# Feed-forward layer behind attention: low parts on VectorE, x split in chunk pairs, high parts first

## Chip, cores and metric

One core of one Trainium2 chip. The metric is the device time of one execution in microseconds (us); 1079.61 us is the median of three runs of the kernel before (1079.18 to 1080.98). Its engines: TensorE (PE, matmuls), VectorE (DVE), ScalarE (ACT), GpSimd (POOL), and SyncE (SP), which issues DMAs.

## The reference

Windowed attention with a few global tokens, then two feed-forward layers over the same 2176 tokens of width 512:

```python
x = attention(q_l, k_l, v_l, q_g, k_g, v_g)      # 4 batches x (32 global + 512 local) tokens, 8 heads x 64
# layer 1 (1536 wide)
xn = x / sqrt(mean(x * x, -1) + 1e-6) * rms_g
g, val = xn @ w_gate, xn @ w_val
x = (g / (1 + exp(-g)) * val) @ w_out
# layer 2 (2048 wide)
h = x @ w_in
P = a[0] + a[1]*h + a[2]*h**2 + a[3]*h**3
Q = 1 + abs(b[0])*abs(h) + abs(b[1])*h**2
out = (P / (Q + 1e-6)) @ w_out2
```

The weights come as 64-bit floats, the rest as 32-bit.

## The kernel before

**Precision.** Each matmul of the two layers is done in a reduced 32-bit format (F32R), three times: high part of the weight by high part of x, low by high, high by low. A high part is a rounding copy on ScalarE, a low part a subtraction (value less high part) on VectorE or GpSimd. TensorE so has three matmuls for each product, lines 618 to 620 for the way up and 645 to 647 for the way down.

**Weights.** `Weights.stages` (line 73) turns a 128x512 tile of 64-bit words into a high and a low part in four stages: ScalarE L83 and L85, VectorE L91, L92 and L95, GpSimd L99 (an add of two 32-bit tiles), then ScalarE L104 and a low part L105 on the engine `lo_eng` that the caller of `step` passes: GpSimd in attention and in layer 2, VectorE between them. A tile is fetched by SyncE one conversion ahead. Twelve tiles of layer 2 are converted in layer 1 and stored to a scratch in DRAM; GpSimd's queue loads them back (L70) when layer 1 is over.

**Layer 1** (`FFN1`) runs as 24 tasks: three groups of 512 of the 1536 middle features, and in each the eight blocks of 288 or 256 tokens (half a batch). A task splits x of its block into four chunk tiles `xt0` to `xt3` of one buffer each, high (L607, ScalarE) and low (L608), then goes through four slices k of 128 features. For each it has `up` of chunks 0 and 1, `up` of chunks 2 and 3 (12 matmuls each, with a `yield` behind: a unit), and `act`: silu or tanh on ScalarE, the product with the value half on VectorE (L633), its high part `ah` (L634, ScalarE) and low part `al` (L636). The way down of the block before (`down`, 12 matmuls for each of four output slices m) stands behind slices 0 and 1; its result goes to `y`, by ScalarE (L651) in group 0, by an addition on VectorE (L653) later. The split for the next task is asked for behind the last `up` of the last slice. Low parts of x are on GpSimd in group 0 and on VectorE in groups 1 and 2; `al` is on GpSimd while the gate is computed with tanh, and on VectorE once silu's table is in use (unit 96 on).

`norm_stages` scales x of a block beforehand; its three adds (L578, L580, L582) are GpSimd's. The eight norms are appended in the attention loop at the ends of steps 4, 8, 14, 18, 22, 26, 30 and 34, and each step takes three stages of them, which is one whole norm.

**Order.** The attention loop (line 854) interleaves the first 60 units with its steps t = 0 to 35: `target` says how many should be done, 7 at the end of step 8, 60 at the end. `between` and the loop behind a step run units up to that. Then the rest of layer 1 runs unit by unit, from unit 72 on with a conversion step behind each. Layer 2 (`ffn2`) follows, with VectorE, ScalarE and GpSimd (L130, L741) in its middle.

The emitted instructions are put in order by a planner that simulates the engines: among the instructions that are ready it takes the one emitted first, and `high_priority(offset=n)` counts an instruction as emitted n places sooner. Each engine runs its instructions in the order so found. PSUM has five banks for `psg` and `psv` behind attention and three for `psA` and the norms.

Of the kernel before, what the change touches and what calls it, by code (L numbers as in the profile page):

```python
# [10 lines left out]
F32 = mybir.dt.float32  # L11
F32R = mybir.dt.float32r
I32 = mybir.dt.int32
U32 = mybir.dt.uint32
AF = mybir.ActivationFunctionType
# [14 lines left out]
NB1 = SG + SL // 2  # L30
# [11 lines left out]
class Weights:  # L42
# [30 lines left out]
    def stages(self, job, lo_eng, r8_act):  # L73
        nc = self.nc
        self.fetch(job)
        key, raw, alloc, _, scratch = job
        v = self.pool.tile([128, 512], I32, tag="cv", name=f"cv{self.n}", bufs=2)
        self.n += 1
        vf = v.bitcast(F32)
        if self.wide:  # L80
            words = raw.rearrange("p a f -> p (a f)").rearrange("p (f w) -> p f w", w=2)
            hi, lo = words[:, :, 1], words[:, :, 0]
            nc.scalar.activation(out=vf, in_=hi.bitcast(F32), func=AF.Abs)  # L83
            if r8_act:
                nc.scalar.activation(out=lo, in_=lo.bitcast(U32), func=AF.Copy, scale=2.0**-29)  # L85
            else:
                nc.gpsimd.tensor_scalar(
                    out=lo, in0=lo.bitcast(U32), scalar1=2.0**-29, scalar2=1.0, op0=ALU.mult, op1=ALU.mult
                )
            yield  # L90
            nc.vector.tensor_scalar(out=vf, in0=vf, scalar1=TINY, scalar2=None, op0=ALU.max)  # L91
            nc.vector.tensor_scalar(  # L92
                out=v, in0=v, scalar1=3, scalar2=0x3FFFFFFF, op0=ALU.logical_shift_left, op1=ALU.bitwise_and
            )
            nc.vector.scalar_tensor_tensor(  # L95
                out=v, in0=hi, scalar=-0x40000000, in1=v, op0=ALU.bitwise_and, op1=ALU.bitwise_or
            )
            yield
            nc.gpsimd.tensor_tensor(out=v, in0=v, in1=lo, op=ALU.add)  # L99
        else:  # L100
            nc.vector.tensor_copy(vf, raw[:, 1].bitcast(F32))
        yield
        out = alloc("w", F32R)
        nc.scalar.activation(out=out[:, 0], in_=vf, func=AF.Copy)  # L104
        lo_eng.tensor_tensor(out=out[:, 1], in0=vf, in1=out[:, 0].bitcast(F32), op=ALU.subtract)  # L105
        if scratch is None:
            self.ready[key] = out
        else:
            nc.sync.dma_start(out=scratch, in_=out.bitcast(I32))
# [424 lines left out]
class FFN1:  # L534
# [4 lines left out]
    LN2H = 0.34657359027997264  # L539

    def __init__(self, tc, pool, x, y, gam, wts):
        self.nc, self.pool, self.x, self.y, self.gam, self.wts = tc.nc, pool, x, y, gam, wts
        nc = self.nc
        self.ones = pool.tile([128, 128], F32, name="ones")
        nc.gpsimd.memset(self.ones, 1.0 / DM)
        self.eps = pool.tile([128, 1], F32, name="eps")
        nc.gpsimd.memset(self.eps, self.LN2H * (127 - 0.0430))
        self.norms = {}
# [21 lines left out]
    def norm_stages(self, blk):  # L570

        nc = self.nc
        nb = self.width(blk)
        t = lambda i: self.pool.tile([128, NB1], F32, tag=f"st{i}", name=f"st{i}_{blk}", bufs=1)[:, :nb]
        m, r, u = t(0), t(1), t(2)
        nc.scalar.activation(out=m, in_=self.xs(blk, 0), func=AF.Square)
        nc.scalar.activation(out=r, in_=self.xs(blk, 1), func=AF.Square)
        nc.gpsimd.tensor_tensor(out=m, in0=m, in1=r, op=ALU.add)  # L578
        nc.scalar.activation(out=u, in_=self.xs(blk, 2), func=AF.Square)
        nc.gpsimd.tensor_tensor(out=m, in0=m, in1=u, op=ALU.add)  # L580
        nc.scalar.activation(out=r, in_=self.xs(blk, 3), func=AF.Square)
        nc.gpsimd.tensor_tensor(out=m, in0=m, in1=r, op=ALU.add)  # L582
        yield
        ps = self.bank(self.acc, f"psN{blk}")
        nc.tensor.matmul(ps[:, :nb], self.ones, m, start=True, stop=True)
        nc.vector.tensor_scalar(out=m, in0=ps[:, :nb], scalar1=1e-6, scalar2=None, op0=ALU.add)
        nc.scalar.activation(out=r, in_=m.bitcast(I32), func=AF.Exp, scale=-self.LN2H / 2**23, bias=self.eps)
        yield
        for up in (1.0 + 1.65e-4, 1.0):
            nc.vector.scalar_tensor_tensor(out=u, in0=r, scalar=-0.5 * up, in1=m, op0=ALU.mult, op1=ALU.mult)  # L590
            nc.vector.tensor_tensor(out=u, in0=u, in1=r, op=ALU.mult)
            nc.vector.scalar_tensor_tensor(out=r, in0=u, scalar=1.5 * up, in1=r, op0=ALU.add, op1=ALU.mult)
        for c in range(4):
            v = self.xs(blk, c)
            nc.vector.scalar_tensor_tensor(out=v, in0=v, scalar=self.gam[:, c : c + 1], in1=r, op0=ALU.mult, op1=ALU.mult)

    def split(self, grp, blk):
        nc = self.nc
        if grp == 0:
            for _ in self.norms[blk]:  # L600
                pass
        lo = nc.gpsimd if grp == 0 else nc.vector
        nb = self.width(blk)
        xt = [self.pool.tile([128, 2, NB1], F32R, tag=f"xt{c}", name=f"xt{grp}_{blk}_{c}", bufs=1)[:, :, :nb] for c in range(4)]
        for c in range(4):
            v = self.xs(blk, c)
            nc.scalar.activation(out=xt[c][:, 0], in_=v, func=AF.Copy)  # L607
            lo.tensor_tensor(out=xt[c][:, 1], in0=v, in1=xt[c][:, 0].bitcast(F32), op=ALU.subtract)  # L608
        return xt

    def up(self, k, blk, xt, cs, pss):
        nc = self.nc
        for c in cs:
            for j in range(2):
                w = self.wts.get(("gv"[j], k))
                wh, wl = (w[:, i, c * 128 : c * 128 + 128] for i in range(2))
                ps = pss[j][:, : self.width(blk)]
                nc.tensor.matmul(ps, wh, xt[c][:, 0], start=(c == 0), stop=False)  # L618
                nc.tensor.matmul(ps, wl, xt[c][:, 0], start=False, stop=False)  # L619
                nc.tensor.matmul(ps, wh, xt[c][:, 1], start=False, stop=(c == 3))  # L620

    def act(self, k, blk, pss, use_silu):
        nc = self.nc
        nb = self.width(blk)
        t = lambda tag, dt, bufs: self.pool.tile([128, NB1], dt, tag=tag, name=f"{tag}{blk}_{k}", bufs=bufs)[:, :nb]
        a, ah, al = t("a", F32, 2), t("ah", F32R, 6), t("al", F32R, 5)
        g, v = pss[0][:, :nb], pss[1][:, :nb]
        if use_silu:
            self.last_silu = nc.scalar.activation(out=a, in_=g, func=AF.Silu)  # L629
        else:  # L630
            nc.scalar.activation(out=a, in_=g, func=AF.Tanh, scale=0.5)
            nc.vector.scalar_tensor_tensor(out=a, in0=a, scalar=1.0, in1=g, op0=ALU.add, op1=ALU.mult)  # L632
        nc.vector.scalar_tensor_tensor(out=a, in0=a, scalar=1.0 if use_silu else 0.5, in1=v, op0=ALU.mult, op1=ALU.mult)  # L633
        nc.scalar.activation(out=ah, in_=a, func=AF.Copy)  # L634
        lo = nc.vector if use_silu else nc.gpsimd
        lo.tensor_tensor(out=al, in0=a, in1=ah.bitcast(F32), op=ALU.subtract)  # L636
        return ah, al

    def down(self, grp, blk, acts, m):
# [15 lines left out]
    def units(self, tasks):  # L655

        prev, xt = None, None
        for i, (grp, blk, use_silu) in enumerate(tasks):
            if xt is None:
                xt = self.split(grp, blk)  # L660
            acts = []
            for kk in range(4):
                k = 4 * grp + kk
                pss = [self.bank(self.gv, f"ps{j}_{blk}_{k}") for j in "gv"]
                self.up(k, blk, xt, (0, 1), pss)
                yield
                self.up(k, blk, xt, (2, 3), pss)
                if kk == 3:
                    xt = self.split(*tasks[i + 1][:2]) if i + 1 < len(tasks) else None
                acts.append(self.act(k, blk, pss, use_silu()))  # L670
                yield
                for m in ((0,), (1, 2, 3), (), ())[kk]:
                    if prev:
                        self.down(*prev, m)
                        yield
            prev = (grp, blk, acts)
        for m in range(4):
            self.down(*prev, m)
            yield
# [89 lines left out]
def kernel(  # L769
# [83 lines left out]
    ffn.set_psum(pp, ("big", banks[0]), ("o", banks[2]))  # L853
    for t in range(LAST + 1):
        if t >= SECOND:
            target[0] = 7 + (IN_ATTN - 7) * (t + 1 - SECOND) / (LAST + 1 - SECOND)
        elif t >= START:
            target[0] = 7 * (t + 1 - START) / (SECOND - START)
        with tc.high_priority(offset=50) if t >= START else nullcontext():
            att.step(t, between)  # L860
        while done[0] < target[0] - 1:
# [25 lines left out]
    wb = left("wb")  # L887
    pp = ps_scope.enter_context(tc.tile_pool(name="ps2", bufs=1, space=PSUM))
    ffn.set_psum(pp, ("gv", 5), ("acc", 3))
    for f in group_loads(1, wb):  # L890
        f()
    norms += [ffn.norm(blk) for blk in ORD if blk not in ffn.norms]
# [80 lines left out]
```

## Time and profile before

| | us |
|---|---|
| median of 3 runs | 1079.61 |
| the profiled execution | 1080.32 |
| its span, first to last instruction | 1078.5 |
| TensorE busy | 1002.8 (93%) |
| VectorE busy | 792.1 (73%) |
| ScalarE busy | 597.6 (55%) |
| GpSimd busy | 368.0 (34%) |

The last output of attention (L413) starts at 307.6 us, the first silu (L629, group 1) at 380.5, the last at 676.7. Busy time is a union over the instructions of an engine, and a matmul counts from its start to a modelled end, so a busy TensorE is not a TensorE at its peak: the row says when it had something to do. [...] In the views of waits, "A <- B" is an idle time of A's engine that ended when B was done. A low mean clock together with a full busy share means that matmuls ran, but slowly.

### The profile page before, as it was taken

Reading aid. Unit: us, or ns where it says so; the run is one execution under the profiler, and the core shown is the slowest. Engines: PE = TensorE matmul, PEld = TensorE weight load, DVE = VectorE, ACT = ScalarE, POOL = GpSimd, SP = SyncE. Lnnn points to the kernel's source line nnn. Section 1 sums busy time; section 2 is a strip of 40 time slices with the busy share of each in tenths; the row PEclk is TensorE's granted clock in tenths of the full one; section 3 lists DMA queues with packets and bytes.
Section 4 is the critical chain, followed back from the end, with each engine's and each line's share of the span. In section 5 each row is a group of like instructions: output and inputs, shape, how many; then the busy total and the mean of one; then the engine's idle time right before and its main releaser. Section 6 shows DMA issues by size and latency. Waiting matters only on the chain.

```text
span 1078.5 us, 23732 instructions
## 1 busy us (share of the span) xinstructions
PE 1002.8 (93%) x9376; PEld 906.2 (84%) x9376; DVE 792.1 (73%) x1754; ACT 597.6 (55%) x1347; POOL 368.0 (34%) x401
## 2 busy tenths in 40 slices
PE   4588999999989989999999999999999999999997
PEld 3366777878878889899989999888989889898895
DVE  3566455565559998863896453799898998989987
ACT  2645454556557664543664242566666666666674
POOL 2445212212227533310331011454353443534443
PEclk8878999999999999999999999999999999999999
DMA  8833545454152422530431013400000000000000
GB/s 220 241 89 70 137 98 122 109 122 92 43 208 87 157 79 78 198 136 2 157 117 41 1 40 118 156 1 1 30 1 30 1 1 30 1 30 2 1 30 20
DMA packets 104047, 83.45 MB, mean 77 GB/s; under 512 B 63360, under 2 KB 91008, under 8 KB 103936
## 3 DMA queue, kind: packets, MB, share of 16 engines
q1 hardware_dynamic: 102208, 75.64, 24.2%
q0 software_dynamic: 1728, 6.29, 1.8%
q8 instruction: 74, 1.21, 0.5%
q14 instruction: 37, 0.30, 0.1%
HBM read 62.64 MB, written 10.75 MB: 68 GB/s over the span
## 4 chain that ended last, share of the span: by engine, by line
PE 38%; DVE 15%; ACT 4%; DMA 2%; issue 2%; POOL 2%; ACTq 0%; POOLq 0%; SPq 0%; DVEq 0%
PE psH L715 4%; PE psH L717 4%; PE psB L750 4%; PE psH L716 4%; PE psB L751 4%; PE psB L752 3%; DVE q L725 2%; PE psg L620 2%; DVE q L737 2%; DVE r L738 2%; PE psg L618 2%; PE psg L619 2%; PE psv L618 2%; PE psv L620 2%; PE psv L619 2%
## 5 line engine op out<-in xcount | busy, mean ns | idle before, releaser
L130 POOL TENSOR_SCALAR gh<-p 128x384 fp32r<-128x384 f32 (+1 forms) x96 | 58.0, 604 | 210.0 <-DVE p L739 179.6
L715 PE MATMUL psH<-yt,w_h 128*128 128x384 f32 (+1 forms) x384 | 126.1, 329 | 0.9 <-ACT yt L697 0.7
L716 PE MATMUL psH<-yt,w_h 128*128 128x384 f32 (+1 forms) x384 | 125.5, 328 | 0.0
L717 PE MATMUL psH<-yt,w_h 128*128 128x384 f32 (+1 forms) x384 | 123.6, 328 | 0.9 <-DVE yt L698 0.9
L645 PE MATMUL psA<-ah,w_o 128*128 128x288 f32 (+1 forms) x384 | 113.8, 298 | 9.1 <-ACT ah L634 3.1
L618 PE MATMUL psg<-xt,w_g 128*128 128x288 f32 (+1 forms) x384 | 115.7, 302 | 5.7 <-ACT xt L607 4.9
L620 PE MATMUL psg<-xt,w_g 128*128 128x288 f32 (+1 forms) x384 | 114.2, 298 | 5.3 <-DVE xt L608 4.7
L618 PE MATMUL psv<-xt,w_v 128*128 128x288 f32 (+1 forms) x384 | 113.5, 296 | 0.5 <-DVE a L632 0.4
L750 PE MATMUL psB<-w_p,gh 128*128 128x512 f32 x272 | 108.2, 398 | 5.5 <-POOL gh L130 5.4
L619 PE MATMUL psg<-xt,w_g 128*128 128x288 f32 (+1 forms) x384 | 112.7, 293 | 0.0
L647 PE MATMUL psA<-al,w_o 128*128 128x288 f32 (+1 forms) x384 | 111.7, 292 | 0.4 <-DVE al L636 0.4
L619 PE MATMUL psv<-xt,w_v 128*128 128x288 f32 (+1 forms) x384 | 112.1, 292 | 0.0
L620 PE MATMUL psv<-xt,w_v 128*128 128x288 f32 (+1 forms) x384 | 111.7, 292 | 0.0
L646 PE MATMUL psA<-ah,w_o 128*128 128x288 f32 (+1 forms) x384 | 111.2, 291 | 0.0
L741 POOL TENSOR_TENSOR gl<-p,gh 128x384 fp32r<-128x384 f32 (+1 forms) x96 | 108.3, 1128 | 8.4 <-PE psB L752 0.4
L751 PE MATMUL psB<-w_p,gh 128*128 128x512 f32 x272 | 107.3, 394 | 0.0
L735 ACT ACTIVATE r<-q,cq 128x384 f32<-128x384 f32 (+1 forms) x96 | 57.4, 598 | 63.9 <-DVE q L725 63.0
L725 DVE SCALAR_TENSOR_TENSOR q<-q,bv,t 128x384 f32<-128x384 f32 (+1 forms) x96 | 69.7, 726 | 21.1 <-ACT q L723 20.9
L645 PEld LDWEIGHTS psA<-ah,w_o 128*128 128x128 f32 x384 | 73.2, 191 | 12.5 <-ACT ah L634 3.8
L752 PE MATMUL psB<-w_p,gl 128*128 128x512 f32 x272 | 82.3, 395 | 0.0
L633 DVE SCALAR_TENSOR_TENSOR a<-a,psv 128x256 f32<-128x256 f32 (+1 forms) x96 | 41.5, 433 | 54.4 <-ACT a L629 47.8
L620 PEld LDWEIGHTS psg<-xt,w_g 128*128 128x128 f32 x384 | 73.8, 192 | 8.9 <-DVE xt L608 6.9
(173 smaller groups left out, 2808.1 us busy)
## 6 DMA issues: line engine op xcount, KB each, us to landing
vw<-vw SPq DMA_DIRECT2D x64, 130.0 KB, 2.5
raw_h<-in_moe_w_in_dram SPq DMA_DIRECT2D x16, 512.0 KB, 3.9
raw_p<-in_moe_w_out_dram SPq DMA_DIRECT2D x16, 512.0 KB, 4.7
raw_g<-in_moe_w_gate_dram SPq DMA_DIRECT2D x12, 512.0 KB, 5.8
raw_v<-in_moe_w_val_dram SPq DMA_DIRECT2D x12, 512.0 KB, 5.6
raw_o<-in_moe_w_out_dram SPq DMA_DIRECT2D x12, 512.0 KB, 8.0
vw<-in_v_l_dram SPq DMA_DIRECT2D x62, 80.0 KB, 2.7
out_dram<-o SPq DMA_DIRECT2D x17, 256.0 KB, 2.0
```

What stands on the lines that cost most here:

```text
L618: nc.tensor.matmul(ps, wh, xt[c][:, 0], start=(c == 0), stop=False)
L619: nc.tensor.matmul(ps, wl, xt[c][:, 0], start=False, stop=False)
L620: nc.tensor.matmul(ps, wh, xt[c][:, 1], start=False, stop=(c == 3))
L645: nc.tensor.matmul(ps, wh, ah, start=(i == 0), stop=False)
L646: nc.tensor.matmul(ps, wl, ah, start=False, stop=False)
L647: nc.tensor.matmul(ps, wh, al, start=False, stop=(i == 3))
L715: nc.tensor.matmul(ph[:, :n], wh, yt[:, c, 0, :n], start=(c == 0), stop=False)
L716: nc.tensor.matmul(ph[:, :n], wl, yt[:, c, 0, :n], start=False, stop=False)
L717: nc.tensor.matmul(ph[:, :n], wh, yt[:, c, 1, :n], start=False, stop=(c == 3))
L750: nc.tensor.matmul(acc[m], gh[:, sl], wh, start=(k == 0), stop=False)
L751: nc.tensor.matmul(acc[m], gh[:, sl], wl, start=False, stop=False)
L752: nc.tensor.matmul(acc[m], gl[:, sl], wh, start=False, stop=(k == NC2 - 1))
```

## The change

`lo_eng` takes the add of a conversion too. `FFN1` has one engine `lo` for its adds and low parts, GpSimd at first, VectorE from the end of attention on. `split` takes a pair of chunks and is called behind each half of the last slice's `up`; in groups 1 and 2 with a priority of 60. `up` has the eight matmuls with the high part of x in front of the four with the low part. The aim for the end of step 8 is 6 units.

```diff
@@ Weights.stages
-            nc.gpsimd.tensor_tensor(out=v, in0=v, in1=lo, op=ALU.add)
+            lo_eng.tensor_tensor(out=v, in0=v, in1=lo, op=ALU.add)
@@ FFN1.__init__
+        self.tc, self.lo = tc, tc.nc.gpsimd
@@ FFN1.norm_stages (three adds alike)
-        nc.gpsimd.tensor_tensor(out=m, in0=m, in1=r, op=ALU.add)
+        self.lo.tensor_tensor(out=m, in0=m, in1=r, op=ALU.add)
@@ FFN1
-    def split(self, grp, blk):
+    def split(self, grp, blk, cs, xt):
         nc = self.nc
         if grp == 0:
             for _ in self.norms[blk]:
                 pass
-        lo = nc.gpsimd if grp == 0 else nc.vector
         nb = self.width(blk)
-        xt = [self.pool.tile([128, 2, NB1], F32R, tag=f"xt{c}", name=f"xt{grp}_{blk}_{c}", bufs=1)[:, :, :nb] for c in range(4)]
-        for c in range(4):
+        for c in cs:
+            xt[c] = t = self.pool.tile([128, 2, NB1], F32R, tag=f"xt{c}", name=f"xt{grp}_{blk}_{c}", bufs=1)[:, :, :nb]
             v = self.xs(blk, c)
-            nc.scalar.activation(out=xt[c][:, 0], in_=v, func=AF.Copy)
-            lo.tensor_tensor(out=xt[c][:, 1], in0=v, in1=xt[c][:, 0].bitcast(F32), op=ALU.subtract)
-        return xt
+            nc.scalar.activation(out=t[:, 0], in_=v, func=AF.Copy)
+            self.lo.tensor_tensor(out=t[:, 1], in0=v, in1=t[:, 0].bitcast(F32), op=ALU.subtract)

     def up(self, k, blk, xt, cs, pss):
         nc = self.nc
+        w = [self.wts.get((j, k)) for j in "gv"]
+        part = lambda j, i, c: w[j][:, i, c * 128 : c * 128 + 128]
+        ps = [p[:, : self.width(blk)] for p in pss]
         for c in cs:
             for j in range(2):
-                w = self.wts.get(("gv"[j], k))
-                wh, wl = (w[:, i, c * 128 : c * 128 + 128] for i in range(2))
-                ps = pss[j][:, : self.width(blk)]
-                nc.tensor.matmul(ps, wh, xt[c][:, 0], start=(c == 0), stop=False)
-                nc.tensor.matmul(ps, wl, xt[c][:, 0], start=False, stop=False)
-                nc.tensor.matmul(ps, wh, xt[c][:, 1], start=False, stop=(c == 3))
+                nc.tensor.matmul(ps[j], part(j, 0, c), xt[c][:, 0], start=(c == 0), stop=False)
+                nc.tensor.matmul(ps[j], part(j, 1, c), xt[c][:, 0], start=False, stop=False)
+        for c in cs:
+            for j in range(2):
+                nc.tensor.matmul(ps[j], part(j, 0, c), xt[c][:, 1], start=False, stop=(c == 3))
@@ FFN1.act
-        lo = nc.vector if use_silu else nc.gpsimd
-        lo.tensor_tensor(out=al, in0=a, in1=ah.bitcast(F32), op=ALU.subtract)
+        self.lo.tensor_tensor(out=al, in0=a, in1=ah.bitcast(F32), op=ALU.subtract)
@@ FFN1.units
             if xt is None:
-                xt = self.split(grp, blk)
-            acts = []
+                xt = {}
+                self.split(grp, blk, range(4), xt)
+            acts, then = [], {}
             for kk in range(4):
                 ...
-                self.up(k, blk, xt, (0, 1), pss)
-                yield
-                self.up(k, blk, xt, (2, 3), pss)
-                if kk == 3:
-                    xt = self.split(*tasks[i + 1][:2]) if i + 1 < len(tasks) else None
-                acts.append(self.act(k, blk, pss, use_silu()))
-                yield
+                for cs in ((0, 1), (2, 3)):
+                    self.up(k, blk, xt, cs, pss)
+                    if kk == 3 and i + 1 < len(tasks):
+                        with self.tc.high_priority(offset=60) if tasks[i + 1][0] else nullcontext():
+                            self.split(*tasks[i + 1][:2], cs, then)
+                    if cs[0] == 2:
+                        acts.append(self.act(k, blk, pss, use_silu()))
+                    yield
                 ...
-            prev = (grp, blk, acts)
+            prev, xt = (grp, blk, acts), then
@@ attention loop
-            target[0] = 7 + (IN_ATTN - 7) * (t + 1 - SECOND) / (LAST + 1 - SECOND)
+            target[0] = 6 + (IN_ATTN - 6) * (t + 1 - SECOND) / (LAST + 1 - SECOND)
         elif t >= START:
-            target[0] = 7 * (t + 1 - START) / (SECOND - START)
+            target[0] = 6 * (t + 1 - START) / (SECOND - START)
@@ behind attention
     ffn.set_psum(pp, ("gv", 5), ("acc", 3))
+    ffn.lo = nc.vector
```

## Rows read from the trace of the kernel before

**Rows 1.** Busy time by stretch: us, engines with counts, clock, DMA share and GB/s.

```profile
320.00:380.00 60.00, 54.80 (x401) 52.25 (x399) 57.04 (x88) 42.55 (x91) 37.76 (x33) 0.97 0.38 134
320.00:480.00 160.00, 148.27 (x1097) 143.35 (x1096) 142.98 (x247) 98.07 (x210) 68.05 (x54) 0.97 0.38 133
580.00:690.00 110.00, 108.13 (x844) 107.38 (x843) 54.15 (x115) 38.03 (x85) 18.84 (x22) 1.00 0.28 84
```

**Rows 2.** Waits of TensorE, 320 to 480 us: total us, times, longest us.

```profile
PE psg L620 <- DVE xt L608: 2.5, 5, 0.8
PE psA L645 <- ACT ah L634: 2.1, 2, 1.1
PE psA L645 <- ACT y L651: 2.0, 1, 2.0
PE psg L618 <- ACT xt L607: 1.5, 2, 1.3
PE psA L645 <- DVE y L653: 1.2, 1, 1.2
PE psg L618 <- DVE a L633: 0.8, 1, 0.8
PE psg L620 <- POOL xt L608: 0.6, 1, 0.6
```

**Rows 3.** Waits of TensorE, 480 to 690 us.

```profile
PE psg L620 <- DVE xt L608: 2.2, 5, 0.6
PE psA L645 <- ACT ah L634: 1.0, 1, 1.0
PE psA L645 <- DVE y L653: 0.6, 2, 0.4
```

**Rows 4.** Busy time of two short stretches, columns as in rows 1.

```profile
327.00:331.00 4.00, 3.88 (x20) 3.88 (x21) 3.86 (x7) 3.73 (x9) 4.00 (x5) 0.61 0.63 235
454.00:457.00 3.00, 2.74 (x13) 2.69 (x13) 2.97 (x6) 2.25 (x6) 0.96 (x1) 0.53 0.50 146
```

**Rows 5.** Single lines, 306 to 692 us: ns min/median/max, first and last start, forms.

```profile
L91 DVE TENSOR_SCALAR cv<-cv x56: 412/428/1584, 312.6 to 679.9; 128x512 f32<-128x512 f32 x56
L105 DVE TENSOR_TENSOR w_v<-cv,w_v x8: 678/688/1810, 323.7 to 399.6; 128x512 fp32r<-128x512 f32 x8
L636 DVE TENSOR_TENSOR al<-a,ah x63: 412/448/1562, 383.9 to 680.2; 128x288 fp32r<-128x288 f32 x32, 128x256 fp32r<-128x256 f32 x31
L633 DVE SCALAR_TENSOR_TENSOR a<-a,psv x74: 407/440/456, 326.6 to 677.1; 128x288 f32<-128x288 f32 x38, 128x256 f32<-128x256 f32 x36
L99 POOL TENSOR_TENSOR cv<-cv,raw_o x8: 1299/1562/1649, 351.9 to 412.6; 128x512 int32<-128x512 int32 x8
```

**Rows 6.** Groups on VectorE, 320 to 480 us: busy us, mean ns, idle before.

```profile
L91 DVE TENSOR_SCALAR cv<-cv 128x512 f32<-128x512 f32 x34 | 23.3, 686 | 11.1 <-ACT cv L83 11.1
L92 DVE TENSOR_SCALAR cv<-cv 128x512 int32<-128x512 int32 x34 | 20.3, 598 | 0.7
L608 DVE TENSOR_TENSOR xt<-x,xt 128x256 fp32r<-128x256 f32 (+1 forms) x24 | 15.7, 665 | 0.0
L636 DVE TENSOR_TENSOR al<-a,ah 128x256 fp32r<-128x256 f32 (+1 forms) x20 | 15.0, 750 | 0.7 <-ACT ah L634 0.5
L105 DVE TENSOR_TENSOR w_v<-cv,w_v 128x512 fp32r<-128x512 f32 x8 | 7.8, 978 | 0.0
```

**Rows 7.** Groups on GpSimd, 320 to 480 us; L99 has five, 34 in all.

```profile
L99 POOL TENSOR_TENSOR cv<-cv,raw_o 128x512 int32<-128x512 int32 x8 | 12.1, 1507 | 12.5 <-DVE cv L95 5.2 <-ACT cv L83 3.4 <-ACT xt L607 2.7
L636 POOL TENSOR_TENSOR al<-a,ah 128x288 fp32r<-128x288 f32 (+1 forms) x12 | 12.0, 1005 | 5.1 <-ACT ah L634 5.1
L608 POOL TENSOR_TENSOR xt<-x,xt 128x256 fp32r<-128x256 f32 (+1 forms) x8 | 7.7, 975 | 0.1
```

**Rows 8.** Timeline of ScalarE at 429.6 us: start, us, instruction, idle before.

```profile
429.64 0.66 ACT L83 ACTIVATE cv<-raw_p 128x512 f32<-128x512 f32 x1 [1.59 <-DMA raw_p<-in_moe_w_out_dram]
430.77 0.40 ACT L634 ACTIVATE ah<-a 128x256 fp32r<-128x256 f32 x1
```

More of the change, by code (lines that the diff above doesn't have):

```diff
@@ L577, in norm_stages @@
         nc.scalar.activation(out=r, in_=self.xs(blk, 1), func=AF.Square)
-        nc.gpsimd.tensor_tensor(out=m, in0=m, in1=r, op=ALU.add)
+        self.lo.tensor_tensor(out=m, in0=m, in1=r, op=ALU.add)
         nc.scalar.activation(out=u, in_=self.xs(blk, 2), func=AF.Square)
-        nc.gpsimd.tensor_tensor(out=m, in0=m, in1=u, op=ALU.add)
+        self.lo.tensor_tensor(out=m, in0=m, in1=u, op=ALU.add)
         nc.scalar.activation(out=r, in_=self.xs(blk, 3), func=AF.Square)
-        nc.gpsimd.tensor_tensor(out=m, in0=m, in1=r, op=ALU.add)
+        self.lo.tensor_tensor(out=m, in0=m, in1=r, op=ALU.add)
         yield
```

## Prediction

> **What bounds the kernel now.** I began with the busy time by stretches. Attention with the first third of the first layer ends near 310 us; the rest of that layer runs to 690 us, the second layer fills what is left. Between 580 and 690 us TensorE is busy 108.1 of 110 us: nothing to gain there. In the same row 844 matmuls take 110 us, 0.13 us each, so a unit of 12 lasts 1.56 us. Between 320 and 480 us it is busy 148.3 of 160 us while VectorE is at 143.0 and GpSimd at 68.1; in its first 60 us VectorE is at 57.0 [rows 1]. TensorE is the bound everywhere behind attention, and what can be won is its idle time plus the half-clock time that follows.
>
> The waits of TensorE come next. From 320 to 480 us it waits for the split of x in three rows (2.5 us for low parts of VectorE, 0.6 for those of GpSimd, 1.5 for the high parts of ScalarE), for y 1.2 us, for the gated product 0.8, for `ah` 2.1, and 2.0 for a copy of y on ScalarE [rows 2]. From 480 to 690 us: 2.2 for low parts, 1.0 for `ah`, 0.6 for y [rows 3]. The reader is to see that the split of x is the largest sum, 2.5 + 0.6 + 1.5 + 2.2 = 6.8 us. [...]
>
> Last, why VectorE is late. Its instructions with two SBUF operands, and the single-source L91, have a median near their minimum and a maximum three times that (L91 412/428/1584 ns, L636 412/448/1562, L105 678/688/1810), while L633, which reads one operand from PSUM, never exceeds 456 ns [rows 5]. So the two engines hold each other up over SBUF operands. As I read it the planner's order stands on times that are then not kept, and a low part of x behind a stretched conversion comes 1 us late.
>
> **The change part by part.** *GpSimd's work to VectorE.* Behind attention `lo_eng` and `self.lo` are VectorE. In 320 to 480 us that moves one L99 for each of the 34 conversions (L91 x34), 12 low parts L636 and 8 low parts L608 [rows 6, 7]. L99 on VectorE is not in the trace; it lies between L91's 0.43 us (same size, one source) and the 1.30 us of its minimum on GpSimd. I take L105's 0.688, a two-source instruction of the same 128x512 [rows 5]. 34 x 0.688 = 23.4 us, with 20 x 0.448 = 9.0 us: 32.4 us added (23.6 to 53.2 by the ends).
>
> What VectorE gets back: mean of the stage less the undisturbed median. L91 34 x (686 - 428) = 8.8 us; L92, same shape, 34 x (598 - 428) = 5.8; L608 24 x (665 - 448) = 5.2; L636 20 x (750 - 448) = 6.0; L105 on w_v 8 x (978 - 688) = 2.3 [rows 5, 6]: 28.1 us. So VectorE goes from 143.0 to 143.0 + 32.4 - 28.1 = 147 of 160 us. It gains no free time; it gains instructions that last what they should, none over 0.7 us where now one lasts 1.8.
>
> [...] If all 68 us of GpSimd's time were VectorE's blocked time, VectorE would fall to 143 + 32 - 68 = 107 us, which would favour the larger gain below; the means give back 28, so I go by those.
>
> *Splitting in pairs, one unit earlier.* The tiles `xt` have one buffer each. Chunks 0 and 1 of the next block are now split once the last up(0, 1) has read them, while up(2, 3) runs for 1.56 us; ScalarE's two high parts and VectorE's two low parts fit (two low parts 0.9 us). In groups 1 and 2 a priority of 60 puts them ahead of conversions. *High parts first.* In a pair 8 matmuls (1.04 us) run before a low part is read, so far two (0.26 us). One conversion of 0.69 us in front of a low part is then covered, a stretched one of 1.8 would not be. Together I let 6.0 of the 6.8 us go. If the cover is gone, because conversions stack up, the 6.8 stay.
>
> *Late products.* y (1.2 + 0.6), the gated product (0.8) and the `ah` behind 480 us (1.0), 3.6 us, wait on VectorE chains with stretched instructions. Half goes: 1.8 us. The bounds are 0 and 3.6.
>
> *Clock.* The stretch at 327 us follows waits for x and for the product, both treated; 1.6 us go. That at 454 us follows `ah` waits of another cause: at 429.6 us ScalarE stands at L83, for a DMA of raw_p, and `ah` is two instructions behind it [rows 8]. Faster conversions don't bring that DMA. The 2.1 us of `ah`, the 1.4 us of clock and the 2.0 us of the y copy stay.
>
> *Fewer units early.* The aim of 7 is 6: the split asks for the next block's norm one unit sooner. One unit may leave slack and come back in a full stretch: 0 to 1.6 us, I take 0.8. More bound work than this doesn't move in attention, but its order is planned anew; I allow 3 us either way.
>
> *At no cost:* the adds of the norms. All eight norms are through their first stage inside the attention loop, before `self.lo` changes. The last matmul on g comes two later (0.26 us); five banks hide it, since bank waits are only the 0.8 us for L633. Were that cover gone, 64 such units in groups 1 and 2 would cost up to 16 us. No DMA changes its place in SP's queue; the scratch stores wait for L105, which comes up to 0.6 us sooner (1.30 - 0.688). On POOL's queue nothing but the twelve reloads stays behind attention until the second layer.
>
> Sum: -6.0 - 1.8 - 1.6 + 0.8 = -8.6 us. The profiled execution took 1080.32 us (span 1078.5 and 1.8 around it), 0.7 above the median, so 1071.7 by itself and **1071.0** beside the median of 1079.61.
>
> **Rivals.** *Larger gain.* All 6.8, all 3.6, both clock stretches (3.0) and the other `ah` waits (2.1) go: -15.5 us, 1064. For it: the waits are small and chained. Against it: the DMA in rows 8.
>
> *The stall only changes its name.* VectorE stays at 147 of 160 us, ScalarE's queue still stops at L83 with `ah` behind; where x no longer waits, `ah` or y is next and takes the time back before 480 us. Left are the 2.2 us behind 480, less 0.8: -1.4, 1078.2. For it: rows 8 and VectorE's load; against it: `ah` has only three waits.
> [...]
>
> *Slower: VectorE is full in 320 to 380 us.* GpSimd has 37.8 of its 68.1 us there [rows 1], 0.555: moved 18.0 us, given back 15.6; 57.0 + 18.0 - 15.6 = 59.4 of 60. If only half comes back it is 67.2, and 7.2 us push TensorE, whose `a`, `al` and low parts stand in that queue; less the 2.2 behind 480 us and the 1.5 for high parts: +3.5, 1083. It decides once less than 15 us come back. Against it: conversions can slide into the roomier 100 us that follow, and the first of group 1's weights have their L105 at 323.7 us [rows 5], while group 0 still runs.
>
> **How the numbers follow.** Forecast 0.50, larger gain 0.15, renamed stall 0.19, slower 0.16. The forecast's own range is 1066 to 1075. To leave out a tenth on either side, the range goes from 1063, just under the larger gain, to 1082.5, inside the slower case. This measurement can tell about 0.2%, 2.2 us. Faster: 0.97 of 0.50, 0.15, and 0.3 of 0.19 = 0.69; slower: 0.9 of 0.16 and 0.1 of 0.19 = 0.16; the rest, 0.15, within.
>
> **What would show it.** Right: between attention and the second layer no GpSimd arithmetic; L91 never above 0.5 us; no wait for `xt` worth over 1 us in sum; full clock at 327 us; VectorE near 147 us in a stage like 320 to 480. The y copy's 2.0 us stays. Wrong: waits for `xt`, `a` or `al` while VectorE has no idle time in the 60 us after attention; or the waits gone and the end of the first layer not earlier; or attention itself ending more than 3 us off.

## The result, and the profile after

The changed kernel takes **1051.85 us** (four runs, 1049.33 to 1053.50) against 1079.39 us of the kernel before on the same chip: ratio 0.9745, 95% interval 0.9725 to 0.9765, a gain of 27.5 us. Forecast were 1071.0, range 1063 to 1082.5. The sign was right; the gain is more than three times the forecast 8.6 us and larger than the "larger gain" rival. The profiled execution of after took 1052.0 us, with a span of 1050.2 us and a mean granted clock, as a share of the full one, of 0.980 (before 0.973). In the code after, x is split in L608 (high) and L609 (low), `up` is L618, L619 (high) and L622 (low), silu L631, `a` L634 and L635, `ah` L636, `al` L637, `down` L646 to L648, y L652 and L654.

Silu starts 17 us earlier after, so the stretches that answer to those from 320 us begin at 303 us. Busy time by stretch, columns as in [rows 1]:

```profile
303.00:363.00 60.00, 59.53 (x459) 59.23 (x458) 53.66 (x121) 45.37 (x97) 0.00 (x0) 0.96 0.55 193
303.00:463.00 160.00, 154.74 (x1209) 153.58 (x1208) 138.50 (x309) 100.44 (x217) 0.00 (x0) 0.98 0.42 145
```

TensorE goes from 148.3 to 154.7 of 160 us and does 1209 matmuls where it did 1097. VectorE has 309 instructions for 247 and yet is busy for less time, 138.5 for 143.0 us. GpSimd does nothing at all in this stretch.

The waits of TensorE after, 303 to 463 us (total us, times, longest), which answer to [rows 2]:

```profile
PE psA L646 <- ACT ah L636: 2.3, 1, 2.3
PE psA L646 <- DVE y L654: 1.6, 2, 0.8
PE psg L618 <- ACT xt L608: 0.8, 1, 0.8
PE psA L646 <- ACT y L652: 0.5, 1, 0.5
```

From 463 to 655 us one row is left of [rows 3]:

```profile
PE psA L646 <- DVE y L654: 0.6, 1, 0.6
```

The waits for x are 0.8 us where there were 6.8. The copy of y on ScalarE, forecast to keep its 2.0 us, costs 0.5; `ah` keeps 2.3; y from the addition on VectorE has 1.6 + 0.6 us where it had 1.2 + 0.6. At 327 us [rows 4] the clock is full:

```profile
327.00:331.00 4.00, 4.00 (x35) 4.00 (x34) 3.46 (x8) 3.34 (x8) 0.00 (x0) 1.00 0.00 0
```

The clock rows of the whole stretch behind attention say more. Before, it falls to half (0.50 to 0.51 in the rows) four times, for 3.4 us each, at 310.8, 327.8, 382.4 and 454.1 us; two of these were counted in the prediction, and these are the other two:

```profile
310.80:314.20 3.40, 3.34 (x16) 3.37 (x17) 1.47 (x4) 2.34 (x5) 0.00 (x0) 0.50 1.06 372
382.40:385.80 3.40, 3.40 (x18) 3.40 (x17) 3.37 (x5) 2.07 (x5) 1.63 (x1) 0.51 0.78 272
```

After, it falls once, for 6.8 us right behind attention, and is full from there to the last silu:

```profile
301.10:307.90 6.80, 5.55 (x22) 4.96 (x23) 3.31 (x8) 3.70 (x7) 0.72 (x1) 0.50 1.02 330
308.00:650.00 342.00, 337.21 (x2675) 336.23 (x2675) 249.80 (x565) 176.93 (x393) 4.95 (x9) 1.00 0.31 107
```

Single lines after, 290 to 655 us (ns min/median/max, first and last start, forms), which answer to [rows 5]; L99 now stands under VectorE:

```profile
L91 DVE TENSOR_SCALAR cv<-cv x56: 415/422/429, 304.9 to 652.8; 128x512 f32<-128x512 f32 x56
L105 DVE TENSOR_TENSOR w_v<-cv,w_v x8: 681/685/693, 315.0 to 390.9; 128x512 fp32r<-128x512 f32 x8
L637 DVE TENSOR_TENSOR al<-a,ah x75: 415/447/694, 310.9 to 653.1; 128x288 fp32r<-128x288 f32 x39, 128x256 fp32r<-128x256 f32 x36
L99 DVE CUSTOM_DVE_ANT_0 cv<-raw_o,cv x8: 682/684/686, 343.0 to 404.6; 128x1024 uint16<-128x1024 uint16 x8
```

The medians are those of before; what is gone is the spread: L91's maximum falls from 1584 to 429 ns, L105's from 1810 to 693. Between the end of attention and the last silu, VectorE has 48 instructions over 1.0 us before and none after. L99 lasts 0.684 us, where I had put 0.688. The groups of VectorE, 303 to 463 us (busy us, mean ns, idle before), against [rows 6]:

```profile
L91 DVE TENSOR_SCALAR cv<-cv 128x512 f32<-128x512 f32 x35 | 14.8, 423 | 10.5 <-ACT cv L83 10.3
L92 DVE TENSOR_SCALAR cv<-cv 128x512 int32<-128x512 int32 x35 | 14.7, 421 | 0.3
L637 DVE TENSOR_TENSOR al<-a,ah 128x288 fp32r<-128x288 f32 (+1 forms) x32 | 13.9, 436 | 1.6 <-ACT ah L636 0.9 <-PE psA L648 0.7
...
L609 DVE TENSOR_TENSOR xt<-x,xt 128x256 fp32r<-128x256 f32 (+1 forms) x32 | 13.6, 434 | 0.4 <-ACT xt L608 0.4
```

**Where the 28.3 us of span went.** I cut each execution at three starts: the last L413 on ScalarE (end of attention), the load of silu's table, 1.3 us ahead of the first silu (end of group 0), and the last silu. By single-line rows of the profiled executions, us:

| kernel | attention ends | silu's table load | last silu | from the last silu to the span's end |
|---|---|---|---|---|
| before | 307.6 | 379.2 | 676.7 | 401.8 |
| after | 300.0 | 362.2 | 649.5 | 400.7 |

Attention gives 7.6 us, the rest of group 0 goes from 71.6 to 62.2 (9.4), groups 1 and 2 from 297.5 to 287.3 (10.2), the end gives 1.1. The second layer itself hardly moved. Up to the end of attention, before has 732 matmuls of the layer and after 720: one unit now stands behind it.

Behind attention the idle rows alone can't pay for this. Between the end of attention and the last silu, before has 24 waits over 0.15 us, 15.9 us idle in all; after has 5, 5.3 us. I measured what they cost as the time from one layer matmul's start to the next, less its undisturbed median (0.133 us for 288 columns, 0.1185 us for 256). That excess is 30.5 us before and 9.3 after, 21.2 less. Before, 19.8 of it stands at the waits themselves, 6.1 in matmuls at the half clock (0.213 us from start to start at 256 columns, 383.4 to 385.5 us) and 4.5 in other matmuls that start late; after, about 6, 2 and less than 1. So there was an excess of 30.5 / 15.9 = 1.9 us for each microsecond of idle row. In after and in the experiments e1, e4, f1 and h1 below the same quotient lies between 1.6 and 2.2.

### The profile page after: what moved, and what is told of

Its sections match the earlier page's. It is cut to its first block, busy times and chain, and to the rows that moved or that the text cites. A ratio compares the mean times of both kernels' runs of the same rounds, so it can differ in the third digit from the quotient of the medians.

```text
span 1050.2 us, 23654 instructions
## 1 busy us (share of the span) xinstructions
PE 987.0 (94%) x9376; PEld 898.4 (86%) x9376; DVE 778.5 (74%) x1828; ACT 593.5 (57%) x1347; POOL 266.4 (25%) x327
## 4 chain that ended last, share of the span: by engine, by line
PE 67%; DVE 16%; ACT 7%; DMA 5%; POOL 2%; issue 2%; SPq 1%; ACTq 0%; POOLq 0%; DVEq 0%
PE psg L618 5%; PE psA L646 4%; PE psv L618 4%; PE psg L622 4%; PE psv L619 4%; PE psg L619 4%; PE psv L622 4%; PE psA L648 4%; PE psA L647 4%; PE psH L718 4%; PE psH L719 4%; PE psH L720 4%; PE psB L753 3%; PE psB L754 3%; PE psB L755 3%; PE psS L357 3%
## 5 line engine op out<-in xcount | busy, mean ns | idle before, releaser
L618 PE MATMUL psg<-xt,w_g 128*128 128x288 f32 (+1 forms) x384 | 114.0, 300 | 6.0 <-ACT xt L608 5.7
L646 PE MATMUL psA<-ah,w_o 128*128 128x288 f32 (+1 forms) x384 | 113.2, 298 | 5.3 <-ACT ah L636 2.3
L618 PE MATMUL psv<-xt,w_v 128*128 128x288 f32 (+1 forms) x384 | 111.2, 292 | 0.0
L619 PE MATMUL psv<-xt,w_v 128*128 128x288 f32 (+1 forms) x384 | 110.9, 291 | 0.0
L619 PE MATMUL psg<-xt,w_g 128*128 128x288 f32 (+1 forms) x384 | 110.3, 290 | 0.0
L648 PE MATMUL psA<-al,w_o 128*128 128x288 f32 (+1 forms) x384 | 109.7, 290 | 0.0
L744 POOL TENSOR_TENSOR gl<-p,gh 128x384 fp32r<-128x384 f32 (+1 forms) x96 | 105.9, 1103 | 8.4 <-PE psB L755 0.4
L622 PE MATMUL psv<-xt,w_v 128*128 128x288 f32 (+1 forms) x384 | 103.8, 291 | 0.0
L622 PE MATMUL psg<-xt,w_g 128*128 128x288 f32 (+1 forms) x384 | 103.3, 291 | 0.0
L618 PEld LDWEIGHTS psg<-xt,w_g 128*128 128x128 f32 x384 | 72.9, 190 | 9.1 <-ACT xt L608 6.4
L646 PEld LDWEIGHTS psA<-ah,w_o 128*128 128x128 f32 x384 | 73.0, 191 | 7.6 <-DVE y L654 2.9
```

The source lines that it names most:

```text
L618: nc.tensor.matmul(ps[j], part(j, 0, c), xt[c][:, 0], start=(c == 0), stop=False)
L619: nc.tensor.matmul(ps[j], part(j, 1, c), xt[c][:, 0], start=False, stop=False)
L622: nc.tensor.matmul(ps[j], part(j, 0, c), xt[c][:, 1], start=False, stop=(c == 3))
L646: nc.tensor.matmul(ps, wh, ah, start=(i == 0), stop=False)
L648: nc.tensor.matmul(ps, wh, al, start=False, stop=(i == 3))
```

## Experiments

Ratios are against the kernel before on the same chip, with the 95% interval. "Excess" is the quantity just defined, from one profiled execution each.

**Each part alone.**

e1_engines, only the moves from GpSimd (the norm adds by `self.lo` too):

```diff
-            nc.gpsimd.tensor_tensor(out=v, in0=v, in1=lo, op=ALU.add)
+            lo_eng.tensor_tensor(out=v, in0=v, in1=lo, op=ALU.add)
-        lo = nc.gpsimd if grp == 0 else nc.vector
+        lo = self.lo
-        lo = nc.vector if use_silu else nc.gpsimd
-        lo.tensor_tensor(out=al, ...)
+        self.lo.tensor_tensor(out=al, ...)
+    ffn.lo = nc.vector
```

> The kernel before with the engine edits alone (L99, low parts of x and al on VectorE behind attention; aim 7, split and order of up as before). Of the 28 us the traces put about 10 into attention (most of them between 58 and 100 us), 9 into the rest of group 0 and 10 into groups 1 and 2. Theory A, GpSimd's hold on VectorE is the cause behind attention: waits for xt, a and y mostly gone from 310 to 690 us, 12 to 20 us faster, 1060 to 1067; attention's end within 2 us of before, since no instruction of it changes. Theory B, earlier split and high parts first give the slack: at most 5 us faster, 1075 or more.

Measured 1057.49 us, 0.9791 (0.9749 to 0.9832): 23 of the 27.5 us from this part alone. Its four runs spread from 1052.08 to 1060.56 us, and the profiled one is the fastest, so its stretches are read with that in mind. Its excess is 7.6 us, and TensorE's waits from 310 to 655 us are these two rows. x is not among them, though it is split and ordered as before:

```profile
PE psA L645 <- ACT ah L635: 2.3, 2, 1.2
PE psA L645 <- DVE y L653: 1.5, 2, 1.1
```

e2_high_first, only `up` with the high parts first:

```diff
+        for c in cs:
+            for j in range(2):
+                nc.tensor.matmul(ps[j], part(j, 0, c), xt[c][:, 1], ...)
```

> The kernel before with the order of up alone (high parts first). Theory A: stretched instructions of VectorE stay, a low part has 0.8 us more time: 2 to 4 us faster, about 1076. Theory B: most waits of low parts (5.3 us) and the clock stretch at 327 us go, 6 to 9 us faster. If the 10 us in attention come from fewer changes between full and tiled matmuls, L413's last start moves from 307.6 us to about 298 here.

It takes 1076.28 us, 0.9961 (0.9938 to 0.9983): 4.2 us faster.

e3_aim6, only the aim of 7 made 6 (both `target` lines):

> The kernel before with the aim of 6 units instead of 7 at the end of step 8 alone. Theory C, attention's 10 us come from the unit that no longer stands between its early steps: 8 to 10 us faster, 1070, all before 110 us. Against it (it is the order of up or of the split): within 2 us of before.

It takes 1077.07 us, 0.9964 (0.9946 to 0.9982): 3.9 us faster, where I had priced 0.8 slower. Its attention ends at 301.2 us, 6.4 sooner than before, and the rest of group 0 takes 75.8 for 71.6 us: most of it is given back.

e4_pairs, pairs split behind their last use, priority and aim 6, with the old `up` and the old engines:

```diff
+                for cs in ((0, 1), (2, 3)):
+                    self.up(k, blk, xt, cs, pss)
+                    if kk == 3 and i + 1 < len(tasks):
+                        ... self.split(*tasks[i + 1][:2], cs, then)
```

> The kernel before with the split in chunk pairs, its priority and the aim of 6 (engines and order of up as before). Theory A: 3 to 5 us faster from 310 us on, 1075, since stretched instructions still sit in front of low parts. Theory B: 7 to 10 us from 310 us on. With theory C 8 to 10 us more in attention.

It takes 1078.71 us, 0.9984 (0.9968 to 1.0): nothing that can be told from no change, though it holds aim 6. The excess is 31.9 us.

**Why the engines matter.** There are two theories: GpSimd holds VectorE up over SBUF operands; or it is the hand-overs to GpSimd, and the order planned around them. h1_dummy_adds is e1_engines, whose order of instructions on TensorE, VectorE and ScalarE it keeps (in the traces VectorE's and ScalarE's are alike to the last one, and TensorE's but for some neighbouring small matmuls of attention), with two GpSimd adds behind each conversion that write to a tile no one reads:

```diff
+    def extra(self, out, lo_eng):
+        h = out[:, 0, :NB1].bitcast(F32)
+        for d in self.dummy if lo_eng is self.nc.vector else []:
+            self.nc.gpsimd.tensor_tensor(out=d, in0=h, in1=h, op=ALU.add)
-        lo_eng.tensor_tensor(out=out[:, 1], ...)
+        lo_eng.tensor_tensor(out=out[:, 1], ...); self.extra(out, lo_eng)
```

> The kernel e1_engines plus two adds of 128x288 on GpSimd behind each conversion between attention and layer 2; they read the finished high part of the weight and write a tile that nobody reads (output unchanged). TensorE, VectorE and ScalarE have the same instructions in the same order as in e1_engines. Theory A1, the loss of before is VectorE and GpSimd holding each other up over SBUF: VectorE's two-operand instructions stretch again to over 1 us and at least half of the 22 us of e1_engines is lost again, 1067 to 1078. Theory A2, the loss of before was the hand-over to a slow third engine and the order planned around it: within 3 us of e1_engines, 1054 to 1060.

It takes 1074.95 us, 0.9942 (0.9909 to 0.9976): 17 of e1_engines' 23 us are lost again, and the two intervals lie clear of each other. Its seven runs spread from 1069.98 to 1080.63 us, and the profiled one, 1070.31, lies near the lower end, as in e1_engines. Busy time from 306 to 650 us (columns as in [rows 1]) is shown first for e1_engines:

```profile
306.00:650.00 344.00, 339.55 (x2677) 338.16 (x2677) 253.33 (x571) 181.21 (x397) 4.74 (x8) 1.00 0.33 112
```

and then for h1_dummy_adds:

```profile
306.00:650.00 344.00, 331.31 (x2544) 324.55 (x2545) 282.53 (x560) 178.69 (x392) 115.24 (x110) 0.99 0.29 102
```

GpSimd is busy for 115 us with work that nothing of the layer needs, and VectorE needs 29 us more for 11 instructions fewer. Two of its lines in h1_dummy_adds, 306 to 672 us (columns as in [rows 5]):

```profile
L91 DVE TENSOR_SCALAR cv<-cv x56: 409/416/891, 310.2 to 670.4; 128x512 f32<-128x512 f32 x56
L105 DVE TENSOR_TENSOR w_p<-cv,w_p x15: 676/819/1159, 429.7 to 624.4; 128x512 fp32r<-128x512 f32 x15
```

and the same two in e1_engines:

```profile
L91 DVE TENSOR_SCALAR cv<-cv x56: 415/420/430, 308.7 to 653.3; 128x512 f32<-128x512 f32 x56
L105 DVE TENSOR_TENSOR w_p<-cv,w_p x15: 679/684/693, 417.5 to 606.9; 128x512 fp32r<-128x512 f32 x15
```

The minima agree; the maxima grow, and the median of this L105 with them. By means over 304 to 660 us, the instructions that read one operand from PSUM keep their length (`a` L634 428 ns for 433 in e1_engines, y L653 428 for 432), while three that read SBUF alone grow (`al` L636 514 for 437, xt L609 492 for 436, L105 on w_p 919 for 685). VectorE has 37 instructions over 1.0 us between the end of attention and the last silu, where e1_engines has none and before 48. ScalarE's instructions keep their length (178.7 us for 392, 181.2 for 397). And the waits of TensorE for x, `a` and `al` come back in h1_dummy_adds; the largest rows, 310 to 672 us:

```profile
PE psA L645 <- DVE y L653: 3.0, 2, 2.5
PE psg L621 <- DVE xt L609: 2.5, 6, 0.8
PE psg L619 <- ACT xt L608: 1.2, 3, 0.7
PE psv L619 <- DVE a L633: 1.2, 1, 1.2
PE psA L647 <- DVE al L636: 1.1, 3, 0.5
```

With the order unchanged, and neither VectorE nor ScalarE waiting for GpSimd in any row of this stretch, the stretched instructions are shown to be the cause of the 17 us. Hand-overs are left with the 6 us that did not come back (3 to 10 by the interval), and whether they cost these is open: between the end of attention and the last silu, ScalarE's L104 waits 22.8 us for GpSimd's L99 before, but in e1_engines it also waits 16.6 us for VectorE's, and in h1_dummy_adds 27.1. The excess of h1_dummy_adds is 23.2 us.

g1_l99_only has only the first changed line of e1_engines, g2_lows_only the rest of it:

> The kernel before with only the conversions' add (L99) on VectorE behind attention; low parts of x and al in the rest of group 0 stay on GpSimd. Theory A1: GpSimd is then silent from 381 us on, so groups 1 and 2 gain their 10 us in full and the rest of group 0 a part of its 13: 12 to 18 us faster, 1062 to 1068. If the low parts on GpSimd cause most of it: under 6 us.

> The kernel before with only the low parts of x and al of the rest of group 0 on VectorE; L99 stays on GpSimd. Theory A1: 20 shorter instructions of GpSimd go of 54 in 320 to 480 us; nothing changes behind 385 us: 2 to 6 us faster, 1074 to 1078.

g1 takes 1061.71 us, 0.9826 (0.9786 to 0.9865), a gain of 19 us; g2 takes 1076.56 us, 0.9962 (0.9943 to 0.9981), a gain of 4.1 us. They add up to e1_engines. The integer add of the conversions is the costly one: 1507 ns on GpSimd [rows 7], 684 on VectorE.

f1_no_engines is after with the engines of before (L99, `al` and the low parts back on GpSimd, `ffn.lo` gone):

> The changed kernel with the engines as before (aim 6, pairs, priority and high parts first stay). If the edits only add: e2_high_first gave 4 us, e4_pairs 2, so 1073 to 1076. If pairs and high parts first need each other, as the prediction had it (6 of 6.8 us of waits for x): waits for xt from 310 to 690 us under 1.5 us and 1068 or less.

It takes 1070.89 us, 0.9918 (0.9889 to 0.9947). Its excess is 25.5 us, and these are the waits of TensorE from 310 to 672 us:

```profile
PE psg L618 <- ACT xt L608: 5.6, 4, 2.5
PE psg L622 <- DVE xt L609: 4.9, 10, 0.8
PE psA L646 <- ACT ah L636: 4.4, 4, 1.7
PE psv L618 <- DVE a L634: 0.2, 1, 0.2
```

With pairs, priority and high parts first all there, x is waited for 10.5 us, more than the 6.8 of before. So these edits do not remove the waits for x; the engines do. What f1 gains comes elsewhere: attention ends at 301.5 us for 307.6, and the excess is 5 us less.

**Which of the other parts count once the engines are moved.** f4_engines_aim6 is e1_engines with aim 6; f5_no_pairs is after with x split as before; f2_no_high_first is after with the old `up`; f6_aim5 is after with 5 for 6 in both `target` lines.

> The kernel before with the engine edits and the aim of 6, without pairs and without high parts first. Engines alone gave 1057.5 and the aim alone 3.7 us (8 us at step 12 of attention, 4 given back behind attention). Theory A1 with C, these two are the whole change: 1050 to 1054, as the changed kernel. If pairs or high parts first still carry part of it: 1056 to 1060.

> The changed kernel without the pairs and their priority (engines, aim 6 and high parts first stay). Theory A1 with C: within 3 us of the changed kernel, 1049 to 1055, and no wait for xt between 310 and 650 us even so. If the earlier split is needed: waits for xt of 2 us or more there, 1056 or more.

> The changed kernel with the old order of up (engines, aim 6, pairs and priority stay). Theory A1 with C: within 3 us of the changed kernel, 1049 to 1055. If high parts first are needed once VectorE has all low parts: waits of the low-part matmuls for xt of 2 us or more, 1056 or more.

> The changed kernel with an aim of 5. If each unit that leaves the first nine steps shortens them (7 to 6 gave 8 to 10 us at step 8), step 8 comes 5 us or more before that of the changed kernel (89.3 us), and the whole is 2 to 5 us faster, 1047 to 1050. If 7 to 6 only happened to fit the planner's order better: within 3 us of the changed kernel or slower.

f4 takes 1052.91 us, 0.9761 (0.9732 to 0.9789); f5 1052.11, 0.9751 (0.9728 to 0.9775); f2 1051.83, 0.9743 (0.9723 to 0.9762). None can be told from after: beside the engines and aim 6, pairs, priority and high parts first are worth nothing that shows here. The waits agree: f4, which has none of the three, has no row for `xt` from 300 to 652 us.

f6 takes 1068.82 us, 0.9902 (0.9879 to 0.9924): one unit fewer costs 17 us, in attention, which ends at 316.4 us for 300.0. So the aim is not a slope. In the order of TensorE's instructions, f6 changes kind more often: kinds are the tiles that matmuls write, with the layer's three counted as one. Timeline of f6_aim5 on TensorE at 88 us (start, us, instruction):

```profile
88.07 0.42 PE L390 MATMUL psO<-vw,pt 128*32 128x65 f32 x2
88.43 0.52 PE L357 MATMUL psS<-kt,qt 64*32 64x96 f32 x2
88.88 0.42 PE L390 MATMUL psO<-vw,pt 128*32 128x65 f32 x2
89.23 0.53 PE L357 MATMUL psS<-kt,qt 64*32 64x96 f32 x2
```

No row here shows a wait, yet each pair starts some 0.4 us behind the last. Between the starts of the eighth and the ninth copy of q (L331), after needs 10.4 us with 16 changes of kind (24 layer and 122 attention matmuls), before 14.7 with 33 (24 and 141), f6 20.0 with 50 (24 and 127). But the granted clock differs too. Busy time of these stretches, of after, before and f6 in this order:

```profile
79.00:89.40 10.40, 8.17 (x149) 6.34 (x147) 9.45 (x25) 7.26 (x18) 6.21 (x6) 1.00 0.31 71
85.50:100.20 14.70, 12.69 (x173) 8.77 (x173) 9.07 (x29) 7.93 (x18) 8.09 (x7) 0.97 0.21 50
78.20:98.20 20.00, 19.23 (x153) 11.92 (x151) 9.52 (x24) 7.22 (x18) 6.28 (x6) 0.71 0.18 42
```

Before against after is 4.3 us more for 17 more changes at nearly the same clock; in f6 the changes and the half clock come together, and the timeline above stands wholly in the half clock (a pair of psO lasts 0.42 us in it, 0.30 in before at 93.2 us, at the full clock).

**What is open in attention.** Theory S says that the number of such changes sets the time of attention, U that the number of units done there does. h2_aim4: 4 for 6 in `target`. h3_in56: `IN_ATTN` 56 for 60. h4_off200: `high_priority(offset=200)` for 50 ahead of `att.step`. h5_no_pairs_off200: f5_no_pairs with the same.

> The changed kernel with an aim of 4. Theory S, attention's length follows the number of changes between kinds of matmul on TensorE (378 before, 365 in the changed kernel, 395 with an aim of 5, up to the last psX in the planned order; about 0.25 us each): here 362, so attention ends within 3 us of the changed kernel, 1049 to 1056. Theory U, too few units early leave TensorE idle and 6 is the best aim: slower than with 5, 1068 or more.

> The changed kernel with 56 instead of 60 units before the end of attention. Theory S: 423 changes, 58 more, about 14 us: attention ends no earlier though 48 matmuls (6 us) less stand in it, and the whole is 10 to 18 us slower, 1062 to 1070. Theory U, only the amount of work counts: attention ends 6 us sooner, the rest grows by as much, within 3 us of the changed kernel.

> The changed kernel with a priority of 200 instead of 50 for the steps of attention. Theory S: 358 changes instead of 365, 1 to 3 us faster, 1049 to 1051. Theory U: no difference beyond 2 us.

> The kernel f5_no_pairs with a priority of 200 for the steps of attention, a candidate for the best version. Theory S: 355 changes instead of 361, 1 to 3 us faster than f5_no_pairs, 1049 to 1051.

| kernel | us | ratio (interval) | attention ends | changes of kind up to the last psX | us at the half clock up to attention's end |
|---|---|---|---|---|---|
| before | 1079.39 | 1 | 307.6 | 382 | 44 |
| after | 1051.85 | 0.9745 (0.9725 to 0.9765) | 300.0 | 370 | 34 |
| h2_aim4 | 1060.18 | 0.9822 (0.9802 to 0.9843) | 307.2 | 367 | 41 |
| f6_aim5 | 1068.82 | 0.9902 (0.9879 to 0.9924) | 316.4 | 400 | 55 |
| h3_in56 | 1071.25 | 0.9926 (0.9901 to 0.9950) | 316.2 | 424 | 44 |
| h4_off200 | 1056.52 | 0.9785 (0.9756 to 0.9813) | 301.2 | 367 | 41 |
| h5_no_pairs_off200 | 1057.67 | 0.9799 (0.9777 to 0.9821) | 305.5 | 364 | 41 |

h3 refutes U: there are fewer layer matmuls in attention (672 for 720), and it ends 16 us later. S has the sign right for large differences (f6, h3) and missed the others: h2 has after's count and is 8 us slower; h4 and h5 were to be 1 to 3 us faster, and h4 is not faster, h5 is slower. The granted clock is a rival that no run here separates from S. If a stretch at the half clock costs up to 0.44 of its length (an estimate from the layer's matmuls of 256 columns, 0.213 us apart at the half clock and 0.1185 at the full), the 10 us less of it give after up to 4.4 of its 7.6 us against before, and the 20 us more cost f6 up to 9 of its 16; whether the alternation lowers the clock is not shown. What sets attention's time stays open. The kernels whose attention part is that of before (e1, g1, g2, h1) also end it anywhere from 303.8 to 307.9 us, with 31 to 41 us at the half clock, so part of this is the execution's own spread. None of these versions beats after.

## Why the prediction was right in sign and wrong in size

**Right.** These signs came: no GpSimd arithmetic in the stages behind attention; L91 never above 0.5 us; full clock at 327 us; waits for x under 1 us; L99 at 0.684 us (0.688 assumed). VectorE is at 138.5 us of its stage where 147 was forecast: L95 (means up to 837 ns before, 684 to 687 after) and the L105 of `w_g` and `w_h` (means 897 and 907 ns before, 688 and 686 after) were stretched too and stand in no term of what it gets back. The slower rival (VectorE full in the first 60 us) did not come: 53.7 us busy, no low part waited for. The renamed stall did not come either, for nothing new took the place of x. `ah` stays, at 2.3 us, and for the reason that was given: ScalarE stands at L83 for a DMA of raw_p, with `ah` two instructions behind. Timeline of after on ScalarE:

```profile
453.57 0.66 ACT L83 ACTIVATE cv<-raw_p 128x512 f32<-128x512 f32 x1 [3.15 <-DMA raw_p<-in_moe_w_out_dram]
454.69 0.40 ACT L636 ACTIVATE ah<-a 128x256 fp32r<-128x256 f32 x1
```

That the two engines hold each other up agrees with the maxima that fall and, in h1_dummy_adds, return (L105: 1.81 us before, 0.69 after, 1.16 in h1_dummy_adds). The extreme that was weighed, all 68 us of GpSimd's time given back to VectorE (107 us), did not come: 138.5 was measured.

**Wrong: the price of a wait.** The step that failed is the sum itself, which put each removed wait at its idle row and added one clock stretch: 6.0 + 1.8 + 1.6 = 9.4 us. The clock terms, 1.6 here and 1.4 among what was to stay, are estimates: the two stretches of [rows 4] times what their mean clock lacks of the full one, 4 x 0.39 and 3 x 0.47. Behind attention, up to the last silu, 19.6 us went; attention, for which no gain was forecast, gave 7.6. Idle fell from 15.9 to 5.3 us behind attention, which the larger-gain rival nearly had, but the excess fell by 21.2. At 1.9 us for each of my 6.0 + 1.8 us the same list gives 15 us, clock included. The rest of the 21.2 lies in what the list kept or left out: the y copy, the clock stretches at 382.4 and 454.1 us, the late starts and the smaller waits. I had read two clock stretches where the trace has four.

**Half right: "Late products. Half goes: 1.8 us".** In idle rows 1.4 of the 3.6 us went, near the forecast, but not evenly: the product `a` (0.8) and the `ah` behind 480 us (1.0) wait no more, while y from VectorE waits 2.2 us where it had 1.8. The return of `a` in h1_dummy_adds fits the stretched instructions as its cause. y still waits with none of them left, so for y they were not the whole cause.

**Wrong: the y copy's 2.0 us and the clock at 454 us that "stay".** The y copy costs 0.5 us, at another place (306 us). Before, its wait ended at 381.3 us, with the copy behind the load of silu's table (1.28 us) on ScalarE; f4, with the engines moved, waits 2.4 us for such a copy at 311 us. So why it shrank is open. The short clock stretch at 454 us, put down to `ah`, stands in the trace before behind waits for `ah` (1.14 us), `al` (0.39) and x (0.26). After, it is gone, though the `ah` wait of 2.3 us falls into this very window (granted clock 1.00 from 450 to 460 us, before 0.83); that a wait brings the half clock on is not shown:

```profile
450.00:460.00 10.00, 7.35 (x56) 6.92 (x54) 5.32 (x13) 3.24 (x7) 0.00 (x0) 1.00 0.68 210
```

**Wrong: "Together I let 6.0 of the 6.8 us go", as the work of pairs and of high parts first.** The size was right, by luck; the reason was not. In f1_no_engines these edits leave 10.5 us of waits for x; in e1_engines, without them, there are none; f2, f4 and f5 lose nothing that shows by leaving them out. I had seen that VectorE's sum would hardly change, and concluded that the engines would win little. The sum was the wrong thing to look at. With the engines of before (f1), low parts on VectorE are waited for 4.9 us though the high parts run first; once the conversions keep their time (e1, L91 at most 430 ns), the old order is early enough.

**Wrong: aim 6 at +0.8, attention within 3 us.** Alone it gave 3.9 us; attention ended 7.6 us sooner in after, some 1.5 of which is the unit that moved behind it. I had costed the unit that leaves and not the interleaving that it changes. The cause stays open: the alternation and the clock are not separated.

**The sum as measured.** The engines give 23 us (L99 19, the lows 4), aim 6 some 4 more (3.9 alone; 4.6 between e1 and f4, whose intervals overlap), the rest nothing that shows: 27, for 27.5.

## What to carry to other kernels

Where two engines stretch each other's instructions, look at the maximum beside the median of each line and at what queues behind, not at the engine's total: here the total hardly moved (143.0 to 138.5 of 160 us) and the move of the engines alone gained 2.1%. Price a wait of a TensorE that is otherwise full at what its matmuls lose around it (in these runs 1.6 to 2.2 times the idle row), and count the small waits and every clock stretch too. When edits come together, run each alone and each left out: three of the five edits here did nothing that showed once the right one was in.

## What the runs showed that I had not expected

- The integer add costs VectorE about half of GpSimd's time or less: L99 lasts 1.3 to 1.65 us on GpSimd [rows 5] and 0.684 us on VectorE, where the row of the trace reads CUSTOM_DVE_ANT_0 over 128x1024 uint16.
- Useless GpSimd adds on 128x288 elements cost the kernel 17 us for 115 us of their own time (h1_dummy_adds). The group of them, from 306 to 640 us, that reads `w_h`:

```profile
L47 POOL TENSOR_TENSOR dummy<-w_h 128x288 f32<-128x288 f32 x30 | 35.3, 1197 | 104.5 <-ACT w_h L104 104.5
```

Their mean is 1197 ns, where the shortest of them took 667 and two lone adds of that shape at the start of the stretch 790 each (L581, L583): the delay goes both ways.
- One unit in the early aim swings the kernel by 17 us (aim 6 to 5), and in the profiled executions all of it stands ahead of attention's end. How much of it is the alternation of attention's matmuls with the layer's, and how much the granted clock, is not shown.
